# Reordering the attention units of the second token parity in a gated mix of attention and GEGLU

## The chip, the cores and the metric

One core of one Trainium2 chip runs the kernel. The metric is the device time of one execution in microseconds. The time before is the median of three runs, 597.56 us (595.99 to 598.31). The profile is of one execution of its own, of 596.87 us.

## The reference

Two branches read the same 2048 tokens of 512 channels, and a gate for each token mixes them:

```python
g = sigmoid((x * gate_w).sum(-1, keepdims=True))
out = g * a + (1 - g) * b
# a: attention of 32 heads of 16 channels
idx = pos[:, None] - arange(8)[None, :] * 2        # 8 keys, every second token back
logits = where(idx >= 0, einsum("bhsd,bhswd->bhsw", q, kg) * scale, -1e9)
o = einsum("bhsw,bhswd->bhsd", softmax(logits), vg)
a = o.reshape(B, S, D) @ wo
# b: GEGLU with 1792 hidden channels
b = (gelu(x @ w_gate) * (x @ w_up)) @ w_down
```

Everything is fp32. Since the attention looks back in steps of two tokens, even and odd tokens never meet in it. The kernel calls the two sets of 1024 tokens the two **parities**.

## The kernel before, in words

**Matmuls.** Every fp32 operand is split into a high and a low part (`split`, `split_by_dma`, `hl` and `hh` for the hidden values and for the attention's outputs), and a product is three matmuls: high by high, low by high, high by low. The products with the input are done in a seven-product scheme, whose sums and differences of operands are made on DVE. All of this is on PE, in one order for each parity: keys and queries (L460), values (L348), then fourteen FFN steps (`gate_up`, L730, and `down`, L777), and the output projection (L1002). The first parity's attention is projected in `out_first`, the second parity's in `finish`.

**Attention.** It is not done on PE. `scores` multiplies keys by queries on DVE (L519) and sums over the head's 16 channels (L522), `softmax` takes maximum, difference, Exp, sum, reciprocal and product (L533 to L544; Exp on ACT at L537, the rest on DVE), and `mix` multiplies the values by the weights (L558), adds eight of them in three additions (L562, L564, L566) and transposes (L571). SP then stores the outputs to DRAM (L573), and `channels` loads them again by channels (L980), splits them (L87 on ACT, L88 on DVE) and hands them to the projection. The work is cut into units of 128 channels (8 heads), four to a parity: units 0 to 3 are the first parity's, units 4 to 7 the second's. `load_kq` loads a unit's keys and queries (L503, L504, L500), `load_slots` in `mix` its values (L503, L504). Keys with queries, values, and the products of L519 and L558 have one buffer each; the logits have two.

**What sets the order.** `attention` is a generator that yields a cost after every DVE step. `pull` is called all through the PE work with a budget, and runs the generator until the budget is spent, so that the attention's instructions are written among the FFN's. They get a priority that stands 150 behind. A scheduler then lays out each engine's queue from these priorities with times of its own, and each engine runs its queue in order. `paced` ties the place of an instruction in the queue to the last matmul written before it; it is no wait on the chip. `need` yields until a key is in `done`: (parity, 0) when the first keys and queries of a parity are stored, (parity, 2) when the others are (`key_one`, in the first two FFN steps), (parity, 1) when the values are. `need_o` spends an unlimited budget until a unit's output is written.

**The order of a unit before.** In `attention`, a unit's `softmax` is followed by the load of the next unit's keys and queries (if they are stored), the load of its own values, its `mix`, and then the next unit's `scores`:

```python
            yield from softmax(*un)
...
            ahead = i and to and (to[0], to[1] // 2 * 2) in done
            if ahead:
                load_kq(*to)
            yield from mix(*un, LOAD if mixed else 0.0)
            done.add((*un, "o"))
...
            if ahead:
                yield from scores(*to)
```

So on DVE the Exp of a unit has nothing of the attention between it and the sum that waits for it, only what the FFN puts there. At the end `finish` projects units 4 to 7 in turn, each as two halves of 512 tokens.

Of the kernel before, what the change touches and what calls it, by code (L numbers as in the profile page):

```python
# [10 lines left out]
F32 = mybir.dt.float32  # L11
# [5 lines left out]
P = 128  # L17
# [3 lines left out]
NP = NT // 2  # L21
# [6 lines left out]
UC = 128  # L28
UH = UC // DH
# [2 lines left out]
BEHIND = 150  # L32
PACE = (1.05, 1.22)
LOAD = 4.0
BT = 4
MASKED = -1e9 * DH ** 0.5
LOWS = (4, 8, 10), (4, 6, 8, 10, 12)
# [8 lines left out]
def tile_gated_mix(ctx: ExitStack, tc: tile.TileContext, xt, wqkv, wff, wo, out):  # L46
    nc = tc.nc
    ctx.enter_context(nc.allow_non_contiguous_dma(reason="rows of 512 bytes"))
    pool = ctx.enter_context(tc.tile_pool(name="sb", bufs=1))
# [46 lines left out]
    for par in range(2):  # L96
# [4 lines left out]
        for u in range(NU):  # L101
            for half in range(2):
                OS[par, u, half] = dram.tile([4, 32, 4, BT * 32], F32, name=f"os{par}{u}{half}")

# [44 lines left out]
    def load_v(*names):  # L149

        if not PLACES:
            t = pool.tile([P, 2 * NP - 1, UC], F32, name="v").rearrange("p a c -> p (a c)")
            u = pool.tile([P, 2, BT * UC], F32, name="tb").rearrange("p a c -> p (a c)")
            PLACES.extend([t[:, i * VW:(i + 1) * VW] for i in range(3)] + [u[:, :VW]])
# [181 lines left out]
    def values(par, bg, step, ks=range(7)):  # L336
# [23 lines left out]
        for k, (a, b) in enumerate((("a11", "b11"), ("a12", "b21"), ("s1", "t1"), ("s4", "b22"), ("s2", "t2"),  # L360
                                    ("s3", "t3"), ("a22", "t4"))):
            if k not in ks:
                continue
            for t in range(BT):
                if k == 0:
# [120 lines left out]
    LG = {}  # L486

    def load_kq(par, u):
        hh, c = divmod(u, 2)
        kq = KQ.pop() if KQ else pool.tile([P, 3 * NP - 1, UC], F32, name="kq")  # L490
        k, q = kq[:, :2 * NP - 1], kq[:, 2 * NP - 1:]
        LG[par, u] = k, q
        if not (par or u):

            nc.gpsimd.memset(k[:1, :NP - 1], 0.0)
            for a, b in (1, P - 15), (P - 15, P):
                nc.sync.dma_start(k[a:b, :NP - 1], k[a - 1:b - 1, NP:])
            return
        load_slots(k, KS[par, hh][c], paced)
        paced(nc.sync.dma_start(q, QS[par, hh][c].rearrange("(p j) d -> p j d", j=NP)))  # L500
# [13 lines left out]
    def scores(par, u):  # L514
        k, q = LG[par, u]
        lg = pool.tile([P, UH, NP, W], F32, name="lg", bufs=2)
        for jj in range(0, NP, 2):
            prod = pool.tile([P, 2, W, UC], F32, name="prod")
            paced(nc.vector.tensor_tensor(prod, spans(k, jj), q[:, jj:jj + 2, None, :].to_broadcast([P, 2, W, UC]),  # L519
                                          op=OP.mult))  # L520
            yield 2.3
            nc.vector.tensor_reduce(two_of(lg, jj), prod.rearrange("p j w (h d) -> p (j w) h d", d=DH), axis=AX.X,  # L522
                                    op=OP.add)
            yield 2.3
        first = lg[:1, :, :NP - 1, :W - 1]
        nc.vector.tensor_tensor(first, first, mask[:1, None, :NP - 1, :W - 1].to_broadcast([1, UH, NP - 1, W - 1]),
                                op=OP.min)
        LG[par, u] = lg

    def softmax(par, u):  # L530
        lg = LG[par, u]
        m = pool.tile([P, UH, NP], F32, name="m")
        nc.vector.tensor_reduce(m, lg, axis=AX.X, op=OP.max)  # L533
        yield 0.7
        nc.vector.tensor_tensor(lg, lg, m[:, :, :, None].to_broadcast([P, UH, NP, W]), op=OP.subtract)
        yield 0.7
        nc.scalar.activation(lg, lg, AF.Exp, scale=DH ** -0.5)  # L537
        nc.vector.tensor_reduce(m, lg, axis=AX.X, op=OP.add)
        yield 0.7
        nc.vector.reciprocal(m, m)  # L540
        if par:
            nc.vector.tensor_tensor(m, m, g[:, par, None, :].to_broadcast([P, UH, NP]), op=OP.mult)
        yield 0.4
        nc.vector.tensor_tensor(lg, lg, m[:, :, :, None].to_broadcast([P, UH, NP, W]), op=OP.mult)  # L544
        yield 0.7

    def mix(par, u, pause):
        lg = LG.pop((par, u))
        hh, c = divmod(u, 2)
        v = pool.tile([P, 2 * NP - 1, UC], F32, name="v")  # L550
        load_slots(v, VS[par, hh][c])
        yield pause
        tb = pool.tile([P, 2, BT * UC], F32, name="tb")
        for jj in range(0, NP, 2):
            if jj % BT == 0:
                o = pool.tile([P, 4, BT, 32], F32, name="o")
            prod = pool.tile([P, 2, W, UC], F32, name="prod")
            paced(nc.vector.tensor_tensor(prod.rearrange("p j w (h d) -> p (j w) h d", d=DH),  # L558
                                          spans(v, jj).rearrange("p j w (h d) -> p j w h d", d=DH),
                                          two_of(lg, jj)[:, :, :, None].to_broadcast([P, 2 * W, UH, DH]), op=OP.mult))  # L560
            yield 2.3
            nc.vector.tensor_tensor(prod[:, :, :4], prod[:, :, :4], prod[:, :, 4:], op=OP.add)  # L562
            yield 1.2
            nc.vector.tensor_tensor(prod[:, :, :2], prod[:, :, :2], prod[:, :, 2:4], op=OP.add)  # L564
            two = [prod[:, :, i].rearrange("p j (b c) -> p b j c", b=4) for i in range(2)]
            nc.vector.tensor_tensor(o[:, :, jj % BT:jj % BT + 2], *two, op=OP.add)  # L566
            yield 1.1

            if jj % BT == BT - 2:
                t = tb[:, jj // BT]  # L570
                nc.vector.transpose(t, o.rearrange("p b t c -> p (b t c)"))  # L571
                for a in range(4):
                    nc.sync.dma_start(OS[par, u, jj // BT][:, :, a].rearrange("b i c -> i b c"),  # L573
                                      t[32 * a:32 * a + 32].rearrange("p (b c) -> p b c", b=4))
                yield 0.7

    done = set()
# [13 lines left out]
    def need(*key):  # L591
        while key not in done:
            yield None

    def attention():
        units = [(0, u) for u in range(NU)] + [(1, u) for u in range(NU)]
        yield from need(0, 0)
        yield from scores(0, 0)
        yield from need(0, 1)
        scored, mixed = 1, False  # L600
        for i, un in enumerate(units):
            if scored == i:
                yield from need(un[0], un[1] // 2 * 2)
                load_kq(*un)
                yield LOAD
                yield from scores(*un)
                scored += 1
                mixed = False
            yield from need(un[0], 1)
            yield from softmax(*un)  # L610


            to = units[scored] if scored < len(units) else None
            ahead = i and to and (to[0], to[1] // 2 * 2) in done
            if ahead:
                load_kq(*to)
            yield from mix(*un, LOAD if mixed else 0.0)
            done.add((*un, "o"))
            mixed = not ahead
            if ahead:  # L620
                yield from scores(*to)
                scored += 1

    fill = attention()
    credit = [0.0]
# [437 lines left out]
    for kc in range(KC):  # L1063
        name, i = ("b11", "b21")[kc // 2], kc % 2
# [223 lines left out]
```

## Time and profile before

| | |
|---|---|
| median of three runs | 597.56 us (595.99 to 598.31) |
| the profiled execution | 596.87 us |
| its span, first to last instruction | 595.1 us |
| granted clock of PE | 0.999 |
| ACT busy | 429.4 us (72%) |
| GpSimd busy | 123.4 us (21%) |
| HBM over the span | 195 GB/s |
| share of the chain that ended last: PE, DMA, DVE, ACT | 90%, 6%, 1%, 1% |

PE, DVE, ACT and POOL stand for the matrix, vector, scalar and GpSimd engines, PEld for PE's weight loads, SP for the engine that issues most DMAs. A row of the timeline gives the start, the duration, the engine, the line of the kernel, the operation with its output and input, and in brackets how long the engine had been idle and what ended that. A row of the waits gives the engine and line that waited, what released it, the total, the number of times and the longest. A row of a tile or line gives the number of instructions, their shortest, median and longest time in ns and the first and last start.

### The profile page before, as it was taken

The numbers are of one execution on the slowest core, as the hardware profiler recorded it, in microseconds if no ns is written. First come the engines' busy times: TensorE is split into PE (matmuls) and PEld (weight loads), VectorE is DVE, ScalarE is ACT, GpSimd is POOL, SyncE is SP. The second block draws the span as 40 slices with busy tenths as digits, with TensorE's granted clock in tenths as the row PEclk, the third lists the DMA queues.
The fourth block names the chain that finished last, engine by engine and source line by source line (L and its number), as shares of the span: only waits on it lengthen the run. The fifth ranks groups of instructions, "written<-read, shape, count | busy, mean of one in ns | idle before, by whom it ended". The sixth has DMA issues, their size and how long they took to land.

```text
span 595.1 us, 8276 instructions
## 1 busy us (share of the span) xinstructions
PE 586.6 (99%) x2743; PEld 488.8 (82%) x2743; DVE 533.3 (90%) x622; ACT 429.4 (72%) x758; POOL 123.4 (21%) x144
## 2 busy tenths in 40 slices
PE   9999999999999999999999999999999999999997
PEld 7889887888888888887788888888888888888885
DVE  6989898999799996999996999799979988999891
ACT  6778786678887779777767665767696778796632
POOL 0130670112111112112001571112121212141200
PEclk9999999999999999999999999999999999999999
DMA  8689999989878988899889999889778988988725
GB/s 301 223 235 295 307 284 236 295 245 243 260 219 246 232 268 234 237 344 267 255 264 330 258 276 227 230 190 265 198 247 213 260 213 215 265 197 230 98 53 176
DMA packets 89464, 143.28 MB, mean 241 GB/s; under 512 B 8655, under 2 KB 49999, under 8 KB 89422
## 3 DMA queue, kind: packets, MB, share of 16 engines
q1 hardware_dynamic: 67470, 106.91, 54.6%
q0 software_dynamic: 21664, 35.46, 33.8%
q8 instruction: 21, 0.34, 0.3%
q10 hardware_dynamic: 288, 0.39, 0.2%
q14 instruction: 21, 0.17, 0.1%
HBM read 69.83 MB, written 46.49 MB: 195 GB/s over the span
## 4 chain that ended last, share of the span: by engine, by line
PE 90%; DMA 6%; DVE 1%; ACT 1%; issue 1%; SPq 0%; ACTq 0%; DVEq 0%
PE p L730 42%; PE p L777 13%; PE acc L777 12%; PE acc L460 10%; PE p L1002 5%; PE acc L348 3%; PE p L348 3%; DMA g<-raw 2%; PE acc L1002 2%; DMA v<-vs 1%; DMA raw<-ws 1%; PE p L460 1%; DMA vs<-hh 1%; DMA raw<-xt 1%; DVE raw L245 1%
## 5 line engine op out<-in xcount | busy, mean ns | idle before, releaser
L730 PE MATMUL p<-S,g 128*128 128x512 f32 x672 | 166.7, 389 | 0.0
L730 PEld LDWEIGHTS p<-S,g 128*128 128x128 f32 x672 | 126.0, 188 | 26.1
L730 PE MATMUL p<-A,g 128*128 128x512 f32 x504 | 125.1, 390 | 0.7 <-DMA g<-raw 0.7
L730 PEld LDWEIGHTS p<-A,g 128*128 128x128 f32 x504 | 94.3, 188 | 20.8 <-DMA g<-raw 1.1
L558 DVE TENSOR_TENSOR prod<-v,lg 128x2048 f32<-128x2048 f32 x32 | 72.9, 2279 | 0.8
L519 DVE TENSOR_TENSOR prod<-kq 128x2048 f32<-128x2048 f32 x32 | 72.9, 2278 | 0.6 <-DMA kq<-kq 0.3
L522 DVE TENSOR_REDUCE lg<-prod 128x128 f32<-128x2048 f32 x32 | 73.0, 2281 | 0.1
L777 PE MATMUL p<-d,hh 128*128 128x512 f32 x224 | 68.8, 389 | 0.0
L689 POOL DMA_DIRECT2D g<-raw x27 | 23.4, 867 | 188.9 <-ACT g L686 122.9
L741 ACT ACTIVATE c<-p 128x512 f32<-128x512 f32 x56 | 33.3, 597 | 38.9 <-PE p L730 38.6
L777 PE MATMUL acc<-d,hh 128*128 128x512 f32 x224 | 58.4, 390 | 0.0
L777 PEld LDWEIGHTS acc<-d,hh 128*128 128x128 f32 x224 | 42.0, 188 | 8.9 <-ACT hh L749 0.2
L777 PEld LDWEIGHTS p<-d,hh 128*128 128x128 f32 x224 | 42.1, 188 | 8.7
L742 DVE TENSOR_TENSOR c<-c,s 128x512 f32<-128x512 f32 x56 | 37.8, 683 | 5.6 <-ACT c L741 5.4
L777 PE MATMUL p<-d,hl 128*128 128x512 f32 x112 | 42.6, 389 | 0.0
L746 DVE TENSOR_TENSOR c<-c 128x512 f32<-128x512 f32 x56 | 38.3, 684 | 3.2 <-ACT c L843 3.1
L562 DVE TENSOR_TENSOR prod<-prod 128x1024 f32<-128x1024 f32 x32 | 39.1, 1221 | 0.3
L735 ACT ACTIVATE s<-p 128x512 f32<-128x512 f32 x56 | 33.0, 590 | 7.1 <-PE p L730 6.5
L721 POOL DMA_DIRECT2D d<-r x23 | 19.7, 858 | 86.6 <-ACT d L720 60.0
L460 PE MATMUL acc<-d,S 128*128 128x512 f32 x144 | 35.2, 390 | 0.6 <-ACT hh L1164 0.6
L790 ACT ACTIVATE rt<-p 128x512 f32<-128x512 f32 x48 | 28.1, 594 | 9.4 <-PE p L777 9.1
L777 PE MATMUL acc<-d,hl 128*128 128x512 f32 x112 | 34.5, 389 | 0.0
(220 smaller groups left out, 1065.0 us busy)
## 6 DMA issues: line engine op xcount, KB each, us to landing
g<-raw POOLq DMA_DIRECT2D x27, 512.0 KB, 6.1
ws<-g SPq DMA_DIRECT2D x14, 768.0 KB, 5.9
g<-ws SPq DMA_DIRECT2D x14, 768.0 KB, 7.0
r<-wff SPq DMA_DIRECT2D x28, 256.0 KB, 4.5
raw<-wff SPq DMA_DIRECT2D x14, 512.0 KB, 4.5
d<-r POOLq DMA_DIRECT2D x23, 256.0 KB, 6.5
ws<-raw SPq DMA_DIRECT2D x14, 384.0 KB, 4.9
raw<-ws SPq DMA_DIRECT2D x14, 384.0 KB, 4.9
```

Of the source, the lines that this page charges most:

```text
L348: LAST[:] = [nc.tensor.matmul(ps[:, :n], x[:, ts], VO[b][w][:, kc * WQ:kc * WQ + n], start=first, stop=(kc == 1 and i == 2), skip_group_ch ...
L460: LAST[:] = [nc.tensor.matmul(ps, x[:, ts], w, start=(start and kc == i == 0), stop=(kc == 1 and i == 2), skip_group_check=True)]
L519: paced(nc.vector.tensor_tensor(prod, spans(k, jj), q[:, jj:jj + 2, None, :].to_broadcast([P, 2, W, UC]), op=OP.mult))
L522: nc.vector.tensor_reduce(two_of(lg, jj), prod.rearrange("p j w (h d) -> p (j w) h d", d=DH), axis=AX.X, op=OP.add)
L558: paced(nc.vector.tensor_tensor(prod.rearrange("p j w (h d) -> p (j w) h d", d=DH), spans(v, jj).rearrange("p j w (h d) -> p j w h d", d=D ...
L562: nc.vector.tensor_tensor(prod[:, :, :4], prod[:, :, :4], prod[:, :, 4:], op=OP.add)
L730: LAST[:] = [nc.tensor.matmul(ps, w_, a_, start=(start and kc == 0 and n == 0), stop=(kc == 1 and n == 2), skip_group_check=True)]
L741: nc.scalar.activation(c, ps, AF.Copy)
L742: nc.vector.tensor_tensor(c, c, s, op=OP.add)
L746: nc.vector.tensor_tensor(ge, ge, up, op=OP.mult)
L777: LAST[:] = [nc.tensor.matmul(pp, a[:, ts], w, start=(i == 0 and n == 0 and gr == 0), stop=(i == 1 and n == 2), skip_group_check=True)]
L1002: LAST[:] = [nc.tensor.matmul(pa, a, b, start=(first and n == 0), stop=(last and n == 2), skip_group_check=True)]
```

## The change

`softmax` is cut in two: `exps` (maximum, difference, Exp) and `shares` (sum, reciprocal, gate, product), each with a small tile `m` of its own. The load of the values leaves `mix` and becomes `load_values`. `attention` is rewritten around them. For units 0 to 3 the order stays as it was. From unit 4 on, if the next unit's keys are stored, the order is: this unit's values are loaded; the next unit's logits, then the load of the keys and queries after those, then the next unit's maximum, difference and Exp; then this unit's mix; then the next unit's sum and normalisation. For unit 4 itself the next unit's keys and queries are loaded ahead of its own maximum. Unit 7 has no next unit: its mix follows unit 6's with only its own sum, normalisation and load of values between. No operation and no transfer is added or taken away.

```diff
+PIPE = 4
...
-    def softmax(par, u):
+    def exps(par, u):
         lg = LG[par, u]
         m = pool.tile([P, UH, NP], F32, name="m")
         nc.vector.tensor_reduce(m, lg, axis=AX.X, op=OP.max)
...
         nc.scalar.activation(lg, lg, AF.Exp, scale=DH ** -0.5)
+
+    def shares(par, u):
+        lg = LG[par, u]
+        m = pool.tile([P, UH, NP], F32, name="m")
         nc.vector.tensor_reduce(m, lg, axis=AX.X, op=OP.add)
...
-    def mix(par, u, pause):
-        lg = LG.pop((par, u))
+    VT = {}
+
+    def load_values(par, u):
         hh, c = divmod(u, 2)
-        v = pool.tile([P, 2 * NP - 1, UC], F32, name="v")
+        VT[par, u] = v = pool.tile([P, 2 * NP - 1, UC], F32, name="v")
         load_slots(v, VS[par, hh][c])
-        yield pause
+
+    def mix(par, u):
+        lg, v = LG.pop((par, u)), VT.pop((par, u))
...
+        scored, ready, shared = [0], [], []
+
+        def keyed(i):
+            return i < len(units) and (units[i][0], units[i][1] // 2 * 2) in done
+
+        def logits(i):
+            if units[i] not in LG:
+                load_kq(*units[i])
+                yield LOAD
+            yield from scores(*units[i])
+            scored.append(i)
+
...
-        scored, mixed = 1, False
+        mixed = False
         for i, un in enumerate(units):
-            if scored == i:
+            if i not in scored:
                 yield from need(un[0], un[1] // 2 * 2)
-                load_kq(*un)
+                yield from logits(i)
+                mixed = False
+            if i not in ready:
+                if i >= PIPE and keyed(i + 1):
+                    load_kq(*units[i + 1])
+                yield from exps(*un)
+            yield from need(un[0], 1)
+            if i not in shared:
+                yield from shares(*un)
+            pipe, ahead = i >= PIPE and keyed(i + 1), i and keyed(i + 1)
+            if not pipe and ahead:
+                load_kq(*units[i + 1])
+            load_values(*un)
+            if pipe:
+                yield from logits(i + 1)
+                if keyed(i + 2):
+                    load_kq(*units[i + 2])
+                yield from exps(*units[i + 1])
+                ready.append(i + 1)
+            elif mixed:
                 yield LOAD
...
-            yield from mix(*un, LOAD if mixed else 0.0)
+            yield from mix(*un)
             done.add((*un, "o"))
             mixed = not ahead
-            if ahead:
-                yield from scores(*to)
-                scored += 1
+            if pipe:
+                yield from shares(*units[i + 1])
+                shared.append(i + 1)
+            elif ahead:
+                yield from logits(i + 1)
```

More of the change, by code (lines that the diff above doesn't have):

```diff
@@ L599, in attention @@
         yield from need(0, 1)
-        scored, mixed = 1, False
+        mixed = False
         for i, un in enumerate(units):
-            if scored == i:
+            if i not in scored:
                 yield from need(un[0], un[1] // 2 * 2)
-                load_kq(*un)
-                yield LOAD
-                yield from scores(*un)
-                scored += 1
[L608 to L614, printed above, removed]
-            if ahead:
-                load_kq(*to)
-            yield from mix(*un, LOAD if mixed else 0.0)
+                yield from logits(i)
[18 more added lines that the diff above has]
+            elif mixed:
+                yield LOAD
+            yield from mix(*un)
             done.add((*un, "o"))
             mixed = not ahead
-            if ahead:
-                yield from scores(*to)
-                scored += 1
+            if pipe:
[3 more added lines that the diff above has]
+                yield from logits(i + 1)
     fill = attention()
```

## Prediction

> **What bounds the kernel now.** I read the page's busy shares first, then the waits of PE, once over the whole span and once from 340 us on, where the second parity's units run, and then the busy time by stretches. The page and the stretches:
>
> ```profile
> span 595.1 us, 8276 instructions
> PE 586.6 (99%) x2743; PEld 488.8 (82%) x2743; DVE 533.3 (90%) x622; ACT 429.4 (72%) x758; POOL 123.4 (21%) x144
> ...
> core 0: us, PE busy (x) PEld busy (x) DVE busy (x) ACT busy (x) POOL busy (x), PEclk, DMA share, GB/s
> 0.00:340.00 340.00, 335.51 (x1637) 281.48 (x1638) 307.97 (x391) 256.31 (x470) 69.99 (x87) 1.00 0.93 264
> 340.00:580.00 240.00, 240.00 (x1059) 198.45 (x1059) 222.66 (x228) 169.45 (x282) 53.44 (x59) 1.00 0.86 212
> 580.00:591.20 11.20, 11.09 (x49) 8.84 (x48) 2.67 (x4) 3.10 (x6) 0.00 (x0) 1.00 0.48 162
> 591.20:595.10 3.90, 0.00 (x0) 0.00 (x0) 0.00 (x0) 0.52 (x1) 0.00 (x0) 0.88 0.56 208
> ```
>
> PE stands still for 595.1 - 586.6 = 8.5 us: 340.00 - 335.51 = 4.5 us lie before 340 us, nothing between 340 and 580, and 3.9 us behind the last matmul, where the last rows of the output are copied and written. The list of PE's waits over the whole span has nine rows, all of them before 340 us; asked for 340 to 592 us, the same view has no row. The first two of the nine are
>
> ```profile
> PE p L73 <- DVE warm L70: 1.0, 1, 1.0
> PE p L730 <- DMA g<-raw: 0.7, 1, 0.7
> ```
>
> A busy PE is not yet a full one, because the ends of matmuls are modelled. So I check it by starts. One piece of the chain of work that ended last is
>
> ```profile
> 478.17 6.80 PE p L730 x30
> ```
>
> 6.80 / 30 = 0.2267 us from start to start in a run of matmuls that wait for nothing. Over the 240 us stretch it is 240 / 1059 = 0.2266. The two agree, so from 340 to 580 us PE starts a matmul whenever it can. **The second parity is bound by PE alone.** DVE is busy for 222.66 of the same 240 us, and half of its idle time there is the wait that this change is about. This is the list of DVE's waits from 340 us on (its first three rows), and then the four sums of the Exp in the timeline:
>
> ```profile
> DVE m L538 <- ACT lg L537: 8.5, 4, 2.7
> DVE hl L88 <- ACT hh L87: 6.4, 1, 6.4
> DVE c L742 <- ACT c L741: 2.5, 3, 1.6
> ...
> 377.31 0.69 DVE L538 TENSOR_REDUCE m<-lg 128x64 f32<-128x512 f32 x1 [1.88 <-ACT lg L537]
> 435.91 0.69 DVE L538 TENSOR_REDUCE m<-lg 128x64 f32<-128x512 f32 x1 [2.71 <-ACT lg L537]
> 492.84 0.69 DVE L538 TENSOR_REDUCE m<-lg 128x64 f32<-128x512 f32 x1 [1.47 <-ACT lg L537]
> 554.80 0.69 DVE L538 TENSOR_REDUCE m<-lg 128x64 f32<-128x512 f32 x1 [2.42 <-ACT lg L537]
> ```
>
> DVE stands 8.5 us for Exp, in four units, and no wait of PE comes of it. That is the core of this prediction: the stall is real, and it is hidden already.
>
> **What is removed.** For units 5, 6 and 7 the sum moves behind a whole mix, so that their waits of 2.71, 1.47 and 2.42 us go: 6.6 us of DVE time. Unit 4 has no mix ahead of it, its sum still follows its Exp, and its 1.88 us stay. On PE this is worth nothing: what is late next is PE itself, at 0.2267 us a matmul. The earlier 4.5 us lie ahead of unit 4 and the last 3.9 us behind the last matmul, so neither is in reach. Taken: 0. The ends of what this term can be: 0, and 6.6 us if all of it reached PE (a rival below).
>
> **What is added.** No engine instruction and no DMA. The second small tile for the sum is a buffer, not an operation. The table loads and Exps stay as many as they were. A unit's logits now lie beside the logits of the unit before it, in the two buffers which that tile already has; the third unit's logits need the first buffer only behind the first unit's mix, on the same engine, so no wait comes of it. Cost 0.
>
> **What is moved: the loads of keys and queries.** Before, unit 5's logits stood behind unit 4's whole mix. Now they follow unit 4's normalisation directly, where the mix began at 381.45 us. The loads, and when they land, from the view of that tile, and the mix's first row:
>
> ```profile
> L503 SPq DMA_DIRECT2D kq<-ks x3: 326/327/365, 371.7 to 482.5; - x3
> L500 SPq DMA_DIRECT2D kq<-qs x3: 430/437/1867, 372.6 to 484.5; - x3
> DMA to landing us min/median/max: 3.3/5.8/10.5
> 381.45 2.29 DVE L558 TENSOR_TENSOR prod<-v,lg 128x2048 f32<-128x2048 f32 x1
> ```
>
> The last of the three was issued at 372.6, so it lands by 378.4 at the median and 383.1 at worst: DVE would wait 0 to 1.7 us. I take 0, and on PE 0 at both ends, since DVE's four waits of 1.47 to 2.71 us in the same place cost PE nothing. For units 6 and 7 a whole mix lies between, some 20 us, and the loads are covered.
>
> **What is moved: the last loads of values.** This is the one edit that can hurt. There is one buffer for values. Before, unit 7's values were loaded when unit 6's mix had read its last, and unit 7's logits, maximum and Exp lay between. Now unit 7's mix follows unit 6's with only a sum and a normalisation between. The end of unit 6's mix, the load behind it and its landing times, the normalisation, and DVE's other work that fell into the Exp stretch before:
>
> ```profile
> 513.62 2.29 DVE L558 TENSOR_TENSOR prod<-v,lg 128x2048 f32<-128x2048 f32 x1
> 517.03 1.22 DVE L562 TENSOR_TENSOR prod<-prod 128x1024 f32<-128x1024 f32 x1
> 518.29 0.69 DVE L564 TENSOR_TENSOR prod<-prod 128x512 f32<-128x512 f32 x1
> 519.01 0.43 DVE L566 TENSOR_TENSOR o<-prod 128x256 f32<-128x256 f32 x1
> 519.47 0.71 DVE L571 STREAM_TRANSPOSE tb<-o 128x512 f32<-128x512 f32 x1
> ...
> 515.94 0.34 SPq L503 DMA_DIRECT2D v<-vs  x1
> 516.33 0.44 SPq L504 DMA_DIRECT2D v<-vs  x1
> DMA to landing us min/median/max: 3.4/4.8/9.2
> ...
> 555.52 0.55 DVE L540 RECIPROCAL m<-m 128x64 f32<-128x64 f32 x1
> 556.11 0.22 DVE L542 TENSOR_TENSOR m<-m,g 128x64 f32<-128x64 f32 x1
> 556.37 0.69 DVE L544 TENSOR_TENSOR lg<-lg,m 128x512 f32<-128x512 f32 x1
> ...
> 549.30 0.68 DVE L750 TENSOR_TENSOR hl<-c,hh 128x512 fp32r<-128x512 f32 x1
> 551.11 1.28 DVE L88 TENSOR_TENSOR hl<-raw,hh 128x512 fp32r<-128x512 f32 x2
> ```
>
> The last read ended at 513.62 + 2.29 = 515.91, and the second half of the load was issued 0.42 us later. It lands 3.4 to 9.2 us after that, so 3.8 to 9.6 us behind the last read, at the median 5.2. The cover is 1.22 + 0.69 + 0.43 + 0.71 = 3.05 us of the mix's end and 0.69 + 0.55 + 0.22 + 0.69 = 2.15 us of sum and normalisation: 5.2 us bare, and about 2 more if the other work above (0.68 + 1.28) stands there again. The new wait is between 0 and 9.6 - 5.2 = 4.4 us. I take 0, the median's value.
>
> Behind that wait DVE holds unit 7's mix and the splits of L88 for the last projection, and PE waits for those. How much room there is, the end of the run shows:
>
> ```profile
> 578.69 0.71 DVE L571 STREAM_TRANSPOSE tb<-o 128x512 f32<-128x512 f32 x1
> ...
> 585.84 0.69 DVE L88 TENSOR_TENSOR hl<-raw,hh 128x512 fp32r<-128x512 f32 x1 [6.44 <-ACT hh L87]
> ...
> 588.66 0.39 PE L1002 MATMUL p<-S,hl 128*128 128x512 f32 x1
> 590.70 0.39 PE L1002 MATMUL p<-S,hl 128*128 128x512 f32 x1
> ```
>
> Unit 7's second half leaves DVE at 579.40, comes back from DRAM, and its low part is split by 585.84 + 0.69 = 586.53. The matmul that first reads it starts at 588.66: 2.1 us of room. With unit 7's own Exp wait of 2.42 us gone from the same chain, the new wait may reach 2.1 + 2.42 = 4.5 us before PE feels it. The worst landing, 4.4 us, just fits. Units 5 and 6 come out later by the time of a unit's logits, but unit 6's projection is not read before 580 us, more than 20 us behind. Cost on PE: 0.
>
> **The sum.** 0 for the waits removed, 0 for the loads, 0 for the order. The profiled execution took 596.87 us, of which the span is 595.1 and 1.8 lie around it. The median of the three runs, 597.56, is 0.7 above it, and I forecast that median: 597.5 us.
>
> **A rule that speaks against "PE is full".** The row is PE at 240.00 of 240 us, with weight loads busy for 198.45, or 83%. The Trainium skill, "Perfetto Trace Analysis", section "Identifying the Most-Contended Engine", says that matmul busy time is no good measure and that the share of weight loads is one. By that share PE would have 17% of the stretch, an estimated 41 us, in which freed DVE time could be turned into matmuls. The starts at 0.2267 us speak against it. The skill's page "TensorE: Matmul & The Clock Gate", section "Wait — 56ns, not 53.3ns?", gives 215.7 ns between starts of warm bf16 matmuls of 512 columns; for these fp32 ones that would be an estimated 1059 x 0.011 = 11.6 us of hidden gaps. No run of such matmuls in the chain is spaced closer than 0.226.
>
> **The rivals.**
> - *Faster: the 6.6 us reach PE.* That needs gaps in PE which the busy rows do not show and which close when DVE runs ahead. The time would be 597.5 - 6.6 = 590.9 us. For it: ends of matmuls are modelled, and the skill's rule on weight loads reads this row so. Against it: equal spacing over 1059 starts and no wait of PE. Chance 0.05.
> - *Slower: unit 7's values come late, because SP stands at another transfer when their buffer comes free.* SP issues in order. In this stretch it issues the loads of the attention's outputs (L980), and they wait for buffers:
>
> ```profile
> SPq L980 <- DMA g<-raw: 9.2, 1, 9.2
> ...
> 544.83 0.79 SPq L980 DMA_DIRECT2D raw<-os  x2
> ```
>
>   If such a 9.2 us wait stood ahead of the values, they would land 9.2 + 5.2 = 14.4 us behind the last read, DVE would wait 14.4 - 5.2 = 9.2, and the end would move by 9.2 - 4.5 = 4.7 us to 602.2. It decides from a wait of DVE over 4.5 us at unit 7's first mix product. For it: one buffer, and SP at L980 in those very microseconds. Against it: the last of these early loads is out by 545.6, and unit 6's last read of values should come at about 546 to 550 (its mix product began behind the normalisation's end, 556.37 + 0.69 = 557.1; less the 2.4 us of the Exp wait, less 5.2 to 7.2 us of cover, and the waits saved before it make it a little earlier). Chance 0.10.
> - *Slower: the new order of DVE's and ACT's queues opens waits of PE in the FFN steps.* The work is cut and placed anew around each piece. If six of the some twelve steps got a wait as long as PE's longest inside the run, 0.7 us, the time would be 597.5 + 4.2 = 601.7. Against it: DVE's and ACT's results feed PE one step later, and DVE's stalls of up to 2.7 us did not come through. Chance 0.07. One or two such waits stay inside the forecast.
> - *The change does not do what it says.* The new order needs the next head half's keys to be stored when unit 5 is at its turn. Counting the budgets in the code, they are complete in the second parity's second FFN step, and unit 4's logits end in the third. If not, the old order stays and so does the time, 597.5. Chance 0.02.
>
> **How the numbers follow.** The forecast has 0.76. A difference of 0.5%, 3.0 us, is about what a measurement of this kernel can tell from no change. Within it lie the forecast and the case without effect, 0.78; faster is the first rival, 0.05; slower are the two others, 0.17. The range goes from 595.3 (the lowest run shown, 595.99, less one PE wait of 0.7) to 601.7, the third rival. Outside stay 0.05 at 590.9 and 0.10 at 602.2.
>
> **What would show it.** If I am right, the waits of L538 for units 5 to 7 are gone, DVE ends unit 7's mix some 2 us sooner or as late as before, PE still has no wait behind 340 us, and the starts stay at 0.2267 us. A row of PE waiting for hh or hl in the last 10 us, with DVE's L558 waiting for v ahead of it, would show the second rival. New rows of PE at L730 or L777 waiting for ACT or DMA would show the third. A span shorter by more than 3 us with no PE wait gone would show that PE had gaps which I could not see.

## The result, and the profile after

The changed kernel took 601.4 us (median of 5 runs, 599.71 to 602.75), against 597.56 us (595.99 to 598.31) before: a ratio of 1.0066 [1.0042, 1.0090], so 2.5 to 5.4 us were lost where I had forecast none. The profiled execution is the one of 602.75 us. Two lines of its page, and its busy times by stretches in the columns of the prediction:

```profile
PE 588.0 (98%) x2743; PEld 489.0 (81%) x2743; DVE 530.5 (88%) x622; ACT 429.8 (72%) x759; POOL 123.5 (21%) x144
PE 86%; DMA 6%; ACT 4%; DVE 2%; issue 1%; SPq 0%; POOL 0%; DVEq 0%; ACTq 0%; POOLq 0%
```

```profile
0.00:340.00 340.00, 333.91 (x1628) 280.09 (x1629) 305.73 (x389) 254.96 (x468) 68.86 (x85) 1.00 0.92 263
340.00:580.00 240.00, 237.12 (x1043) 195.20 (x1042) 222.01 (x230) 171.22 (x286) 54.60 (x59) 1.00 0.87 215
```

Two things are to be seen. ACT has 759 instructions instead of 758, and its share of the chain rose from 1% to 4%. And from 340 to 580 us PE started 1043 matmuls where it had started 1059. At 0.2267 us a start, 16 missing starts are 3.6 us, which is the size of the loss. I use this count below, because it is more complete than the list of waits: in a group of six that takes 1.65 us instead of 1.52, a matmul behind the first waited too, and the row calls that busy.

The 1.6 us between 335.51 and 333.91 are another matter. On every engine the instructions stand in the same order as before up to 368 us, where SP's loads of unit 5's keys come sooner, and a second profile of the changed kernel has 335.21 there. That part is one execution's scatter.

From 340 us on, PE's list of waits had no row before the change. Now it has three. Behind them, from the timeline, the two longest as PE's matmuls show them, the first with the six matmuls ahead of it:

```profile
PE p L762 <- ACT c L773: 1.4, 1, 1.4
PE p L1034 <- ACT c L773: 0.9, 1, 0.9
PE p L809 <- ACT p L803: 0.6, 1, 0.6
```

```profile
465.06 1.52 PE L762 MATMUL p<-A,g 128*128 128x512 f32 x6
467.96 1.20 PE L762 MATMUL p<-A,g 128*128 128x512 f32 x4 [1.38 <-ACT c L773]
...
542.26 1.65 PE L1034 MATMUL p<-g,A 128*128 128x512 f32 x6 [0.90 <-ACT c L773]
```

All three are released by ACT. L773 (before: L741) copies a product `p` out of PE's accumulators, and PE can't write the next product there until the copy is through; L803, in the third, puts an earlier sum back into one. So the next question is what ACT did ahead of those copies. First its timeline around 468 us, at unit 6's Exp, and around 520 to 542 us, at unit 7's:

```profile
463.45 0.60 ACT L773 ACTIVATE c<-p 128x512 f32<-128x512 f32 x1 [4.58 <-PE p L762]
...
465.50 1.28 ACT L540 ACT_TABLE_LOAD   x1
466.79 0.63 ACT L540 ACTIVATE lg<-lg 128x512 f32<-128x512 f32 x1
467.33 0.58 ACT L773 ACTIVATE c<-p 128x512 f32<-128x512 f32 x1
...
520.71 1.28 ACT L540 ACT_TABLE_LOAD   x1
522.00 0.63 ACT L540 ACTIVATE lg<-lg 128x512 f32<-128x512 f32 x1
...
532.66 1.28 ACT L875 ACT_TABLE_LOAD   x1
533.95 0.60 ACT L875 ACTIVATE c<-p 128x512 f32<-128x512 f32 x1
...
541.60 1.09 ACT L773 ACTIVATE c<-p 128x512 f32<-128x512 f32 x2
```

Unit 6's Exp and its table load stand between two copies, and the second of them, at 467.33, is the one that PE waits for. Unit 7's Exp has moved from behind the last Gelu to a place ahead of the last two, so the Gelu at 533.95 needs its table again: that is the 759th instruction. The same engine before the change, at units 5, 6 and 7, and PE's matmul behind unit 6's Exp:

```profile
431.29 0.60 ACT L741 ACTIVATE c<-p 128x512 f32<-128x512 f32 x1 [0.27 <-PE p L730]
...
433.95 1.28 ACT L537 ACT_TABLE_LOAD   x1
...
489.32 0.60 ACT L741 ACTIVATE c<-p 128x512 f32<-128x512 f32 x1 [3.07 <-PE p L730]
...
490.88 1.28 ACT L537 ACT_TABLE_LOAD   x1
492.71 0.58 ACT L741 ACTIVATE c<-p 128x512 f32<-128x512 f32 x1
...
552.85 1.28 ACT L537 ACT_TABLE_LOAD   x1
```

```profile
492.97 2.88 PE L730 MATMUL p<-A,g 128*128 128x512 f32 x12
```

Unit 5's Exp stood behind both copies, and unit 7's behind the last of all these copies, which began at 537.2. Unit 6's stood between two copies, as it does now, and yet PE did not wait (the row of twelve matmuls has no bracket), because PE had more to do before it wanted the second copy. By starts, it was nine matmuls of L777 from 490.93 on and the first six of the twelve, 15 x 0.2267 = 3.4 us; the copy was through at 492.71 + 0.58 = 493.29, 1.0 us ahead of the second six. In the changed kernel the Exp falls into another FFN step, where PE has one matmul of L809 and the six at 465.06, 7 x 0.2267 = 1.6 us. So what counts is what ACT does ahead of a copy and how soon PE wants that copy.

For DVE the change did what it was meant to: of 8.5 us of waits for Exp 1.8 are left. They are unit 7's, though, and not unit 4's. The scheduler set unit 7's sum behind the first of the four products of unit 6's mix, not behind the whole mix; and the first logits of unit 5 now lie between unit 4's Exp and its sum. Unit 7's mix ends earlier than before (575.53 against 579.40), though the kernel ends later:

```profile
513.53 2.27 DVE L568 TENSOR_TENSOR prod<-v,lg 128x2048 f32<-128x2048 f32 x1
...
522.67 0.69 DVE L545 TENSOR_REDUCE m<-lg 128x64 f32<-128x512 f32 x1 [1.79 <-ACT lg L540]
523.27 2.28 DVE L568 TENSOR_TENSOR prod<-v,lg 128x2048 f32<-128x2048 f32 x1
```

### The profile page after: what moved, and what is told of

The parts are those of the page before. It is cut to its first block, busy times and chain, and to the rows that moved or that the text cites. A ratio compares the mean times of both kernels' runs of the same rounds, so it can differ in the third digit from the quotient of the medians.

```text
span 601.0 us, 8284 instructions
## 1 busy us (share of the span) xinstructions
PE 588.0 (98%) x2743; PEld 489.0 (81%) x2743; DVE 530.5 (88%) x622; ACT 429.8 (72%) x759; POOL 123.5 (21%) x144
## 4 chain that ended last, share of the span: by engine, by line
PE 86%; DMA 6%; ACT 4%; DVE 2%; issue 1%; SPq 0%; POOL 0%; DVEq 0%; ACTq 0%; POOLq 0%
PE p L762 39%; PE p L809 12%; PE acc L809 12%; PE acc L463 8%; PE p L1034 5%; PE p L351 3%; PE acc L351 3%; DMA qs<-tb 2%; PE acc L1034 2%; DMA g<-raw 2%; DMA vs<-hl 1%; PE p L463 1%; DMA raw<-xt 1%; DVE raw L248 1%; ACT A L90 1%
## 5 line engine op out<-in xcount | busy, mean ns | idle before, releaser
L762 PE MATMUL p<-S,g 128*128 128x512 f32 x672 | 166.7, 389 | 0.0
L762 PEld LDWEIGHTS p<-S,g 128*128 128x128 f32 x672 | 126.0, 188 | 26.1
L762 PE MATMUL p<-A,g 128*128 128x512 f32 x504 | 126.0, 390 | 3.1 <-DMA g<-raw 1.7
L762 PEld LDWEIGHTS p<-A,g 128*128 128x128 f32 x504 | 94.2, 188 | 23.6 <-DMA g<-raw 2.1
L809 PE MATMUL p<-d,hh 128*128 128x512 f32 x224 | 68.3, 390 | 0.6 <-ACT p L803 0.6
L773 ACT ACTIVATE c<-p 128x512 f32<-128x512 f32 x56 | 33.2, 598 | 40.7 <-PE p L762 33.1
L809 PE MATMUL acc<-d,hh 128*128 128x512 f32 x224 | 58.9, 389 | 0.0
L809 PEld LDWEIGHTS p<-d,hh 128*128 128x128 f32 x224 | 42.0, 188 | 9.7 <-ACT p L803 1.0
L809 PEld LDWEIGHTS acc<-d,hh 128*128 128x128 f32 x224 | 42.0, 188 | 8.8
L809 PE MATMUL p<-d,hl 128*128 128x512 f32 x112 | 42.6, 389 | 0.0
L809 PE MATMUL acc<-d,hl 128*128 128x512 f32 x112 | 34.1, 390 | 0.0
```

The costliest lines, as they stand in the source:

```text
L762: LAST[:] = [nc.tensor.matmul(ps, w_, a_, start=(start and kc == 0 and n == 0), stop=(kc == 1 and n == 2), skip_group_check=True)]
L773: nc.scalar.activation(c, ps, AF.Copy)
L809: LAST[:] = [nc.tensor.matmul(pp, a[:, ts], w, start=(i == 0 and n == 0 and gr == 0), stop=(i == 1 and n == 2), skip_group_check=True)]
```

## The experiments

Four theories. **A**: the loss is ACT's queue; Exps with their table loads delay the copies that PE waits for. **B**: it is the new order of DVE's queue. **C**: it is the new order of SP's loads. **D**, formed on the way: a load of values that now flies beside another transfer. PE's own order has changed too: from 382 us on, matmuls of L809 (before: L777) stand at other places among those of L762. That is a rival to A without a kernel of its own, but four of the kernels below (`e_copy`, `b_copy` and the two of `e_dose`) leave PE's order just as it is in the kernel that they start from, `e_p6copy` leaves that of `e_pipe6`, and `e_late67v` settles it for unit 6. All results, with "before" as measured on the same chip, and the starts of matmuls from 340 to 580 us in the profiled execution (before: 1059):

| kernel | us | before | ratio | starts |
|---|---|---|---|---|
| `after_again` (changed kernel) | 601.31 | 597.11 | 1.0078 [1.0052, 1.0105] | 1043 |
| `e_copy` | 598.60 | 597.47 | 1.0027 [1.0003, 1.0051] | 1041 |
| `b_copy` | 597.43 | 597.47 | 1.0004 [0.9979, 1.0028] | 1059 |
| `e_pipe6` | 601.55 | 597.47 | 1.0067 [1.0043, 1.0092] | 1039 |
| `e_first2` | 606.31 | 597.47 | 1.0145 [1.0109, 1.0181] | 1020 |
| `e_p6late` | 598.19 | 597.32 | 1.0012 [0.9993, 1.0030] | 1059 |
| `e_p6copy` | 597.80 | 597.32 | 1.0005 [0.9985, 1.0025] | 1057 |
| `e_dose12` | 599.67 | 597.32 | 1.0039 [1.0019, 1.0058] | 1051 |
| `e_dose9` | 600.38 | 597.32 | 1.0045 [1.0025, 1.0065] | 1050 |
| `e_late7` | 601.14 | 597.11 | 1.0065 [1.0044, 1.0086] | 1046 |
| `e_late7_again` | 599.93 | 597.66 | 1.0055 [1.0031, 1.0078] | 1046 |
| `e_late7v` | 600.47 | 597.66 | 1.0051 [1.0029, 1.0073] | 1043 |
| `e_late67` | 599.01 | 597.92 | 1.0018 [1.0002, 1.0034] | 1053 |
| `e_late67v` | 597.26 | 597.31 | 1.0001 [0.9990, 1.0013] | 1057 |

### Without the table loads: `e_copy` and `b_copy`

In the changed kernel and in the one before, the second parity's Exp becomes a Copy, which needs no table of its own (12 table loads are left of 20 and 19). The order of every queue stays.

```diff
-        nc.scalar.activation(lg, lg, AF.Exp, scale=DH ** -0.5)
+        nc.scalar.activation(lg, lg, AF.Copy if par else AF.Exp, scale=DH ** -0.5)
```

> The changed kernel with Copy in place of Exp in the second parity. It leaves out that Exp; the queues of all engines stay as they are, but for eight loads of activation tables that go from ACT (8 x 1.28 = 10.3 us of ACT). Theory A (ACT bounds the bad stretches: the Exps with their table loads stand ahead of the copies that free PE's banks): PE's waits for ACT behind 340 us, 2.9 us in the profile, mostly go, and the time comes to 597 to 598.5 us, within 0.3% of before. Theory B (DVE's new order delays the FFN's additions): nothing changes, about 601 us. Theory C (SP's new order holds loads back, and ACT waits 3.4 us for the attention's outputs): the late waits stay, 600 us or more.

> The kernel before with the same replacement of Exp by Copy in the second parity (that Exp is left out), which takes seven table loads from ACT and changes no queue otherwise. Theory A: in the kernel before no PE wait hung on them, so 597 to 598 us, the same as before within 0.2%. If table loads had been costing PE time everywhere, it would fall below 596 us. Theories B and C expect 597.5 us too.

In the kernel before it is worth nothing (1.0004). In the changed one most of the loss goes at the median, with the order of PE, DVE and SP unchanged, which speaks for A; its interval still touches that of the changed kernel. What remains, 1.1 us [0.2, 3.0], I can't place from its profile: that execution, 602.9 us, is the longest of its twelve. It lost as many starts as the changed kernel (1041), and its waits are for transfers (2.6 us for `hl`) and, in the last projection, for another row of ACT (0.7 us), not for L773.

### The new order from a later unit: `e_pipe6` and `e_first2`

`e_pipe6` takes the new order only from unit 6 on, `e_first2` only at units 4 and 5.

```diff
-PIPE = 4
+PIPE = 6            # e_pipe6
+PIPE = 4, 5         # e_first2, with "i in PIPE" for "i >= PIPE"
```

> The new order only from unit 6 on: units 4 and 5 as before, unit 7's logits, maximum and Exp ahead of unit 6's mix. Theory A: unit 7's Exp now stands among the last FFN steps, where ACT also splits the output weights and the first outputs, with an eighth table load behind it; that stretch shows 0.6 + 0.9 = 1.5 us of PE waits in the changed kernel, so 1.5 to 2.5 us over before, 599 to 600 us. Theory B: one of three reordered units, a third of the loss, 598.8 us. Theory C: all of the loss, since the late loads are moved here, 600.5 to 601.5 us.

> The new order for units 4 and 5 as the leading ones, and the old one at the end: unit 7's logits behind unit 6's mix. Theory A: the wait of 1.4 us at 468 us stays and the late ones go, 598.5 to 599.5 us. Theory B: two of three reordered units, 600.1 us. Theory C: as before, 597.5 us.

In `e_pipe6` only unit 7 is moved, and the whole loss is there already: 601.55 us, which is C's number and not A's. PE's row shows how, with the same reload of the Gelu table ahead of it on ACT:

```profile
538.53 2.93 PE L1034 MATMUL p<-g,A 128*128 128x512 f32 x6 [2.34 <-ACT c L773]
```

2.34 us ahead of the group and 2.93 - 1.52 = 1.41 us inside it make 3.75 us. So the losses at units 6 and 7 do not add up: unit 7 alone costs as much as both, within the intervals. `e_first2` missed everything expected. With unit 7 in the old order, the mixes of units 5 and 6 follow each other in the middle of the FFN, with one buffer for values. Its timeline of DVE and SP:

```profile
481.54 2.29 DVE L568 TENSOR_TENSOR prod<-v,lg 128x2048 f32<-128x2048 f32 x1
...
497.06 2.29 DVE L568 TENSOR_TENSOR prod<-v,lg 128x2048 f32<-128x2048 f32 x1 [7.98 <-DMA v<-vs]
...
485.68 0.38 SPq L506 DMA_DIRECT2D v<-vs  x1
486.10 0.45 SPq L507 DMA_DIRECT2D v<-vs  x1
```

The last read ended at 483.83; SP issued the load 1.9 and 2.3 us later, behind loads of keys. Its second half landed 10.9 us after its issue. DVE waited 7.98 us, and PE 4.3 us (at L809, for `hh` of L786) through the hidden values that DVE and ACT then made late. The wait is of the kind that the prediction priced for unit 7's values (0 to 4.4 us), here at unit 6's; only some 2 us of it are SP's, so the long stand of SP in the second rival is not what this run shows. No kernel with a second buffer for values was run.

### Unit 7's Exp put back or taken out: `e_p6late` and `e_p6copy`

`e_p6late` is `e_pipe6` with unit 7's Exp behind the last Gelu on ACT; `e_p6copy` is `e_pipe6` with the Copy of above.

```diff
+        if (par, u) != LATE:                      # LATE = 1, NU - 1
             nc.scalar.activation(lg, lg, AF.Exp, scale=DH ** -0.5)
...
     def shares(par, u):
+        if (par, u) == LATE:
+            yield from need("first")              # done ahead of out_first's call
+            paced(nc.scalar.activation(lg, lg, AF.Exp, scale=DH ** -0.5))
```

> The kernel with the new order from unit 6 on (e_pipe6), with one thing moved: unit 7's Exp and its table load stand on ACT behind the last Gelu instead of at the head of the last FFN steps. SP's and GpSimd's queues stay as in e_pipe6, PE's too but for the order of three matmuls; DVE keeps unit 7's logits ahead of unit 6's mix, and only unit 7's sum and normalisation follow later. The reload for the last Gelus goes. Theory A (ACT's queue in that stretch): the PE wait for the copy of L773, 2.3 us in e_pipe6, goes, and the time comes to 597 to 598.5 us. Theories B (DVE's order) and C (SP's order): it stays at 601 to 602 us.

> The kernel with the new order from unit 6 on (e_pipe6), with Copy in place of Exp in the second parity (that Exp is left out): eight table loads go from ACT, every other queue stays. Theory A: of the 3.2 us that stood in the stretch 0.6 stay, and the time comes to 597.5 to 599 us. Theories B and C: 601 to 602 us.

Both take the loss away. SP's and POOL's orders are those of `e_pipe6` in both, and in `e_p6copy` DVE's and PE's are too. The stretch in `e_p6late`:

```profile
340.00:580.00 240.00, 239.99 (x1059) 198.13 (x1058) 221.03 (x228) 169.45 (x282) 53.08 (x58) 1.00 0.86 213
```

1059 starts, and no wait of PE. For this end of the run B and C fall, and PE's order with them.

### An Exp added to the kernel before: `e_dose12` and `e_dose9`

One Exp of 4 elements a partition is added ahead of an FFN step, at 524 us (`e_dose12`) or three steps earlier (`e_dose9`). With it come two table loads; nothing else of the order changes.

```diff
+    def extra():
+        paced(nc.scalar.activation(z[:, 0, :4], z[:, 0, :4], AF.Exp))
...
+            if par and f == 12:                   # e_dose9: 9
+                at(7, extra)
```

> The kernel before with one more Exp, of 128 x 4 elements of a tile that is no longer used, put on ACT at the head of the last FFN steps, where the changed kernel has unit 7's Exp. It brings its table load and the Gelus' reload, 2 x 1.28 us, and changes no other queue. Theory A: the stretch of ACT from 523 to 538 us, which ran without a pause before, becomes some 2.8 us longer, PE waits for the copies at its end, and the time is 599 to 601 us. Theories B and C: 597.5 us, as before.

> The same additional Exp with its two table loads three FFN steps earlier in the kernel before, near 475 us, in a step where ACT waits for PE for some 2 us. Theory A: ACT makes the time up in that wait, and the time stays within 0.5 us of before, 597 to 598 us. If two table loads cost PE time wherever they stand, 599 to 601 us as in the other place.

```profile
PE p L1007 <- ACT c L741: 1.8, 1, 1.8
```

At 524 us the old order of PE, DVE and SP loses 2.35 us, at the same copy as the changed kernel. This makes the loss from ACT alone (DVE is as full as ACT in that stretch, but nothing was added to it). `e_dose9` was expected to be covered and was not; its PE waits for something else, by the list of waits, and the timeline of ACT and POOL, below it two rows of ACT in the kernel before, shows why:

```profile
PE acc L777 <- DMA d<-r: 2.0, 1, 2.0
```

```profile
478.46 0.60 ACT L741 ACTIVATE c<-p 128x512 f32<-128x512 f32 x1 [0.99 <-PE p L730]
...
487.80 0.63 ACT L720 ACTIVATE d<-r 128x512 fp32r<-128x512 f32 x1
488.72 0.86 POOL L721 DMA_DIRECT2D d<-r  x1 [0.67 <-ACT d L720]
```

```profile
475.49 0.60 ACT L741 ACTIVATE c<-p 128x512 f32<-128x512 f32 x1 [0.99 <-PE p L730]
...
483.37 0.63 ACT L720 ACTIVATE d<-r 128x512 fp32r<-128x512 f32 x1
```

The copy ahead of the added Exp is 3.0 us later here, which this execution lost earlier and for other reasons. The ACT instruction at 487.80 is 4.4 us later than before, so the added Exp with its loads makes some 1.5 us of that. POOL issues the transfer behind it, and that took 12.3 us to land against 10.4 before, 1.9 us more. PE felt the two together. So the rows of ACT that feed POOL's transfers are a second way from ACT to PE; why the transfer took longer is not shown.

### The changed kernel with unit 7's Exp put back: `e_late7`, twice, and `after_again`

`e_late7` is the edit of `e_p6late` in the changed kernel itself, with the new order from unit 4.

> The changed kernel with one part undone: unit 7's Exp, with its table load, stands behind the last Gelu on ACT again, as it did before the change, and so there is one table load less; unit 6's Exp and the rest of the new order stay. A (ACT's queue): the late waits of PE behind 520 us go (0.6 and 0.9 us in the changed kernel's profile), the 1.4 us at 468 us behind unit 6's Exp stays or not, as ACT happens to stand there: 598.0 to 599.5 us. B (the order of DVE's queue) and C (the order of SP's loads): the mixes and the loads stand as in the changed kernel up to unit 6, so most of the loss stays, 600.5 to 601.5.

> The changed kernel unaltered, on the same chip as the one above, to set its loss beside it: all theories 600.5 to 602 us, and in the profile PE's waits for ACT's copies of the hidden values at about 468 and 542 us.

> The kernel with unit 7's Exp behind the last Gelu, unaltered, for a second profile and on the same chip as the one above: 600.5 to 601.5 us. D: the profile shows PE waiting longer than 0.2 us for the low parts of the last projection's weights if this execution is an average one. A alone: 1.4 us behind unit 6's Exp and no more than 0.5 us elsewhere behind 340 us, however long the execution is.

`after_again` repeats the result. `e_late7` missed what A expected: 601.14 us, which is the number of B and C, then 599.93 on another chip, between the two; a loss of 4.0 and 2.3 us. The two intervals overlap with that of the changed kernel, so the times don't show a gain; the starts are three more (1046 in both profiles against 1043 in both), 0.7 us. Its waits:

```profile
PE p L768 <- ACT c L779: 1.4, 1, 1.4
PE p L1041 <- ACT c L779: 0.5, 1, 0.5
PE p L1041 <- DMA S<-raw: 0.2, 1, 0.2
```

The first is unit 6's Exp, unmoved; it stands with 1.38 us in all five profiles of this order that still had it. The last is new: the low parts of the last projection's weights land late. In the second profile it is 0.4 us, as D expected. Two things were left to take apart, and each got a kernel.

### The values later: `e_late7v`

```diff
-        load_slots(v, VS[par, hh][c])
+        load_slots(v, VS[par, hh][c], *[paced] * ((par, u) == LATE))
```

> The kernel with unit 7's Exp behind the last Gelu, and in addition the load of unit 7's values placed behind the loads of the attention's outputs on SP, so that it no longer flies beside the low parts of the last projection's weights (these landed in 6.4 to 7.3 us there, beside the values, against 3.2 to 4.4 in the kernel before and the changed one, and one matmul of the last projection waited 0.2 us for them). D (what is left of the loss in the kernel with the late Exp is that transfer, which is later in other executions than in the profiled one): they land in 3 to 4.5 us again, no wait of PE for S, and the time falls to 598.5 to 599.5 us, the 1.4 us behind unit 6's Exp being what remains. A alone (the loss is unit 6's Exp and what it sets off): no gain, 600.5 to 601.5 us.

The transfer did what D said (landing in 3.6 to 3.8 us, no wait for `S`), the time did not: 600.47 us, as A alone had it, with the 1.4 us behind unit 6's Exp still there and 1.0 us for a transfer of `hl` in its place. Alone it was no cure.

### Unit 6's Exp later too: `e_late67` and `e_late67v`

`e_late67` is `e_late7` with unit 6's Exp written half a mix later; `e_late67v` adds the edit of `e_late7v`.

```diff
+        if (par, u) == (1, NU - 2):
+            HELD.append(lg)
...
+            if HELD and jj == 4:                  # in mix, behind the first addition
+                lg6 = HELD.pop()
+                paced(nc.scalar.activation(lg6, lg6, AF.Exp, scale=DH ** -0.5))
```

> The kernel with unit 7's Exp behind the last Gelu, and in addition unit 6's Exp half a mix later on ACT (written behind the third product of unit 5's mix), so that it no longer stands ahead of the copy that PE waited 1.4 us for at 465 to 468 us; the new order of logits, mixes and loads stays. A (ACT's queue is the whole cause): that wait goes, and with it nearly all of the loss, 597.3 to 598.9 us. Rest (the new order of DVE's and SP's queues costs something by itself): the wait goes and 1.5 us or more stays, 599.3 us or above.

> The kernel with the Exps of units 6 and 7 both later on ACT, and in addition the load of unit 7's values behind the loads of the attention's outputs on SP. The one wait of PE behind 340 us that the kernel without this had is 1.3 us for the low part of the last projection's weights, which flew beside the values. D (that transfer is the 1.1 us that were left): the wait goes, 597.5 to 598.4 us, no difference from before. Rest (the new order costs something that the waits don't show): 598.7 us or more, though no wait of PE behind 340 us is left.

With both Exps moved no wait of PE for ACT is left, and 1.1 us [0.1, 2.0] of the loss, just between the two ranges expected. They are in one row of PE's. It stands here from the timeline of `e_late67` with SP's load of the values, and below it are the issues and landing times of the tile `S`:

```profile
540.41 0.50 PE L1046 MATMUL p<-S,A 128*128 128x512 f32 x1 [1.30 <-DMA S<-raw]
...
533.43 0.34 SPq L506 DMA_DIRECT2D v<-vs  x1
```

```profile
L226 POOL DMA_DIRECT2D S<-raw x2: 849/854/858, 531.9 to 533.0; - x2
DMA to landing us min/median/max: 3.4/5.4/7.4
```

And `e_late67v`, where the values go at 544.15: the landing of the same tile, the stretch from 340 us on, and the page's line of busy times. The last two rows are ACT's and PE's at the step in which the changed kernel waited for the second copy:

```profile
DMA to landing us min/median/max: 3.2/3.4/3.6
```

```profile
340.00:580.00 240.00, 239.55 (x1057) 198.22 (x1056) 220.26 (x229) 170.46 (x284) 52.78 (x58) 1.00 0.86 213
```

```profile
PE 586.6 (99%) x2743; PEld 489.1 (82%) x2743; DVE 531.0 (89%) x622; ACT 430.1 (72%) x759; POOL 123.4 (21%) x144
```

```profile
463.24 0.60 ACT L784 ACTIVATE c<-p 128x512 f32<-128x512 f32 x1
...
462.94 2.88 PE L773 MATMUL p<-A,g 128*128 128x512 f32 x12
```

597.26 us, a little under D's range, and a ratio of 1.0001 [0.9990, 1.0013]: the new order of logits and mixes, with the Exps and sums of units 6 and 7 and the values of unit 7 later, and no loss that this can tell. One wait of PE is left behind 340 us, 0.5 us for a transfer of `hl`. In the step shown PE's order is that of the changed kernel, the second copy no longer has an Exp ahead of it, and PE goes through its twelve matmuls without a wait: PE's new order alone does not make the loss. ACT has 759 instructions here too, as many table loads as in the changed kernel. So the additional load is not the price by itself; it is where ACT stands at the Exps when PE needs a copy. No kernel beat the one before, and `b_copy` says that there was nothing to win on this side.

## Why the prediction was wrong, point by point

- **What bounds the kernel: right.** PE is full behind 340 us, so a wait there comes out at the end. 16 starts lost at 0.2267 us are 3.6 us; measured were 3.8 and 4.2.
- **The rule against it: it fell.** The Trainium skill, "Perfetto Trace Analysis", section "Identifying the Most-Contended Engine", would have left PE room by its share of weight loads. The traces do not agree: in `e_late67v` DVE's waits for Exp behind 340 us are down from 8.5 to 1.3 us, PE started no more matmuls (1057 against 1059), and the time stayed. That is the test of the first rival too.
- **What is removed: right in its size, in part by luck.** 6.7 us of DVE's waits went where 6.6 were forecast, but they were those of units 4, 5 and 6; unit 7's stayed, because its sum did not move behind a whole mix. PE gained nothing.
- **What is added: wrong in its words.** "The table loads and Exps stay as many as they were" was not so: one load came on top. `e_late67v` has it too and loses nothing, so this error alone was not the cause.
- **The loads of keys and queries: right, the wait's size by luck.** It came, 1.09 us, inside the range of 0 to 1.7, and PE did not feel it. But the loads went out at 368.60 to 369.47 and not up to 372.6, and DVE wanted them at 375.3 and not at 381.45.

```profile
376.40 2.29 DVE L522 TENSOR_TENSOR prod<-kq 128x2048 f32<-128x2048 f32 x1 [1.09 <-DMA kq<-qs]
```

- **The last loads of values: right in the changed kernel, by luck in part.** DVE did not wait for them. SP did stand at other loads (L1012), as the second rival had it, between the two halves: the second went out 6.0 us behind the last read at 539.69, not 0.42 us, and landed 6.1 us later, 0.6 us before DVE's product at 552.44. And the step priced only DVE's wait for that load, not what the load does to others in flight. In `e_late67` that cost PE 1.3 us; in the changed kernel the first half came after those weights were issued at 537.37 and 538.41, and they still landed in 3.2 to 4.3 us.

```profile
539.72 0.34 SPq L506 DMA_DIRECT2D v<-vs  x1
542.78 2.89 SPq L1012 DMA_DIRECT2D raw<-os  x4
545.71 0.51 SPq L507 DMA_DIRECT2D v<-vs  x1
```

- **"0 for the order": this is the step that failed.** The list of what is moved had the loads in it, but not the Exps, though the Exp moves with the maximum and drags 1.28 us of table load along ACT's queue. I dismissed the third rival because "DVE's and ACT's results feed PE one step later, and DVE's stalls of up to 2.7 us did not come through". For DVE that held. ACT also empties PE's accumulators, and those copies are wanted within the step. So the 0 was wrong on ACT's queue: PE's waits for ACT came to 1.4, 0.9 and 0.6 us, and the kernel lost 3.8 us. The rival's sign showed as I had written it, in new rows of PE at those two lines (now L762 and L809) that wait for ACT, and its time, 601.7, was near by luck (it came from six waits of 0.7 us, there were three); its chance of 0.07 was too low. The rows of before would have told it. In the stretch that unit 7's Exp was moved ahead of, ACT had no room, and the weight load of the next projection already waited 0.2 us for a copy (the second row is from the view of L741, who waited for it):

```profile
523.40:537.90 14.50, 14.50 (x66) 11.90 (x65) 14.45 (x12) 14.44 (x29) 5.95 (x7) 1.00 0.92 199
```

```profile
  PEld p L1002: 0.2, 1
```

ACT is busy for 14.44 us of 14.50. An Exp of 0.63 us and two loads of 1.28 are 3.2 us put into or ahead of a full queue that ends in a copy without slack. ACT's 72% over the span had hidden that.

What stays open: `e_copy`'s remaining 1.1 us, and by how much the two Exps' costs overlap. `e_late7`, with only unit 7's Exp put back, still loses 2.3 to 4.0 us, `e_pipe6`, with only unit 7's moved, 4.1, and both together cost 3.8 to 4.2. A PE that is late at 468 us gives ACT that much more time before 540, which would explain it; no run isolates this.

## What to carry to other kernels

When an edit moves an instruction to another place in a queue, price that queue around the new place, not by the engine's share of the span: look for the copies behind it that another engine waits for, how much that engine has left to do until it wants them, and for how long the queue has run without a pause. An Exp among Gelus costs its table load and a second one for the next Gelu, whatever its own size. Where the bound engine is full, count its starts in a fixed stretch; the list of waits shows only part of what was lost.

## What the runs showed of the hardware

- A table load took 1.28 us each time, and the Exp behind it started 0.01 us after its end (465.50 + 1.28, then 466.79). The Trainium skill, "ScalarE: Activation LUTs", section "What ACT_TABLE_LOAD costs", gives the same 1283 ns and about 1380 ns of draining on top. The load agrees; the drain does not appear here as time between the rows, neither behind the load nor ahead of it, where the last row before this one ended at 465.48.
- A load on one queue can hold up a transfer on another: the low parts of the weights landed in 3.2 to 3.6 us without the values beside them (`e_late67v`) and in up to 7.4 us when the values were issued 0.4 us behind the second of them (`e_late67`). Nothing else of the two queues' order differs between these kernels up to there.
- The losses of two delays on one queue were not the sum of the two: 4.1 us with unit 7's Exp alone moved, 3.8 and 4.2 with unit 6's as well.
